# FFT convolution, one core: the inverse transform of the last two blocks with 84 stationary columns instead of 56

## The chip, the cores and the metric

One core of one Trainium2 chip. The metric is the device time of one execution in microseconds; the figures given are medians of a few executions. One further execution is recorded by the hardware profiler; its trace gives the durations and starts used below.

## The reference

A circular 7 x 7 convolution of a 224 x 224 image with 96 input and 96 output channels, written with Fourier transforms:

```
H = W = 224;  C = 96;  K = 7
x: bfloat16 (1, H, W, C);  w: bfloat16 (K, K, C, C)
wp = pad(w, to H x W)
Xf = rfft2(x, axes=(1, 2));  Wf = rfft2(wp, axes=(0, 1))      # float32
Yf = einsum('bhwi,hwio->bhwo', Xf, Wf)
y  = irfft2(Yf, s=(H, W), axes=(1, 2)).astype(bfloat16)
```

## The kernel before

The kernel does not transform the whole image. It cuts the 224 rows into NJ = 8 blocks of B = 28 rows with a halo of 6 (L = 34), and takes a short transform along the rows of each block: NS = 17 frequencies, with a real and an imaginary part, so FR = 34 numbers for each block, column and channel. Along the other axis it convolves directly. The 224 columns are done in NT = 7 tiles of 32 columns. Three kinds of work are TensorE's:

- Forward transform (`a_bank`, `f_jobs`): matmuls `pb<-Fm,xn`, 118 rows of pixels against the matrix Fm.
- The products in frequency space (`b_round`, one call for each tile and frequency): matmuls `pb<-WF,J` and `pb<-WF,xf`, 96 x 128 stationary, 96 columns of weights moving, 3,773 of them. DVE forms the operands J ahead of them (`jit`), ACT and DVE take the results out of PSUM (tiles `tt__`, `u`, `v`), POOL or DVE sum them into `yf`, and SP stores yf into a scratch tensor in DRAM (`scr`).
- Inverse transform (`c_jobs`): the scratch is read back with blocks and frequencies on the partitions (`load_t`, tiles tt), and multiplied by the inverse matrix G (named Gm in the profile). G is 102 x 84: three blocks of 34 rows by three blocks of 28 columns, zero outside the three blocks on the diagonal. ACT or DVE evict the result to a tile yo or to a part of J that is free by then, and SP writes it to the output.

The eight blocks do not divide by three. A tile has five groups (`LT`): blocks 0 to 2 and 3 to 5, each in two halves of 16 columns (gi = 0, 1), and the last two blocks, 6 and 7 (gi = 2). The last group is cut in three jobs, q = 0, 1, 2. In q = 0 and 1 the third block's place is filled with more columns of blocks 6 and 7, so these have three blocks; q = 2 has two blocks alone (`nj = 2`). Each job is a pair of matmuls (b = 0, 1), each into a PSUM bank of its own, and each followed by an eviction.

Before the change such a pair with nj = 2 loads `G[0:68, 0:56]`, 68 rows and 56 columns, and writes 56 rows of the bank. All other pairs of `c_jobs` load `G[0:102, 0:84]`. There are six pairs of the first kind, one for each of the tiles 0 to 5 (the last tile takes another way, with a matrix GY), and 60 of the second.

The order on each engine is the order in which the program issues (`_Ordered` chains the instructions of an engine). The jobs of the inverse transform are dealt out between the products of later tiles by `pace`, by the list `CQ`; most stand between a forward transform and the next products. All PSUM tiles come from eight banks in turn (`bank`). `evac` chooses ACT or DVE by a running sum of estimated costs (`load`), from the number of moving columns, not from the rows.

All instructions go through one helper line, so the profile shows line 88 for nearly all of them; the tiles' names and the shapes tell them apart.

Of the kernel before, what the change touches and what calls it, by code (L numbers as in the profile page):

```python
# [14 lines left out]
B = 28  # L15
# [40 lines left out]
def kernel(  # L56
# [7 lines left out]
    _, H, W, C = x.shape  # L64
# [6 lines left out]
    FR = 2 * NS  # L71
# [23 lines left out]
    VE, SE, GE, TE, DE = (_Ordered(e) for e in (nc.vector, nc.scalar, nc.gpsimd, nc.tensor, nc.sync))  # L95
# [9 lines left out]
    def bank():  # L105
        return pools["psb"].tile([128, 512], F32, name="pb")
# [12 lines left out]
    def evac(out_ap, in_ap, n):  # L119
        if tail[0]:  # L120
            return tail_evac(out_ap, in_ap, n)
        cv, ca = 180 + 1.0 * n, 160 + 0.85 * n
        if load["v"] + cv <= load["a"] + ca:
            load["v"] += cv
            return VE.tensor_copy(out=out_ap, in_=in_ap)
        load["a"] += ca
        return SE.copy(out=out_ap, in_=in_ap)

    def tail_evac(out_ap, in_ap, n):
        tail[0] += 1  # L130
        return VE.tensor_copy(out=out_ap, in_=in_ap) if tail[0] % 2 else SE.copy(out=out_ap, in_=in_ap)

    def dma(out_ap, in_ap):
        return DE.dma_start(out=out_ap, in_=in_ap)
# [7 lines left out]
    G = cpool.tile([3 * FR, 3 * B], BF16, name="Gm")  # L142
# [558 lines left out]
    def new_yo():  # L701
        nyo[0] += 1
        if nyo[0] % 4 > 1:
            return yo_free[nyo[0] % 4 - 2]
        return yo_pool.tile([4 * B, PXC * C], BF16, name="yo")

    def c_jobs(t):
        jobs = []
        w0 = t * 2 * TW
        for gi, h in LT:  # L710
            hold = {}
            nq = 2 if gi < 2 else 3

            def mk_(q, gi=gi, h=h, nq=nq, hold=hold):
                def put(j0, nj, px, npx, row, col):
                    dma(out[0, j0 * B:(j0 + nj) * B, w0 + px:w0 + px + npx, :].rearrange("h w c -> h (w c)"),
                        hold["yo"][row:row + nj * B, col:col + npx * C])

                def f():
                    if q % 2 == 0:  # L720
                        hold["yo"] = new_yo()
                    tt = tt_tiles[(t, gi, h)]
                    yo = hold["yo"]
                    nj = 2 if q == 2 else 3
                    for b in range(2):
                        pb = bank()[0:nj * B, 0:4 * C]
                        TE.matmul(pb, lhsT=G[0:nj * FR, 0:nj * B],
                                  rhs=tt[0:nj * FR, 4 * q + 2 * b:4 * q + 2 * b + 2, :].rearrange("p w e -> p (w e)"), start=True, stop=True)
                        k = 2 * (q % 2) + b
                        evac(yo[0:nj * B, k * 4 * C:(k + 1) * 4 * C], pb, 4 * C)  # L730
                    if q == 1 and gi < 2:
                        put(gi * 3, 3, h * PXC, PXC, 0, 0)
                    elif q == 1:
                        put(6, 2, 0, 16, 0, 0)
                        for j in range(2):
                            put(6 + j, 1, 24, 8, 2 * B, j * 8 * C)
                    elif q == 2:
                        put(6, 2, 16, 8, 0, 0)
                    if q == nq - 1:
                        held[gi == 2] -= 1  # L740
                        pump()
                return f
            for q in range(nq):
                jobs.append(mk_(q))
        return jobs
# [6 lines left out]
    def pump():  # L752
        while pend and held[pend[0][1] == 2] < (NTT, 1)[pend[0][1] == 2]:
            held[pend[0][1] == 2] += 1
            load_t(*pend.pop(0))
# [176 lines left out]
    for i, (j, h) in enumerate(order):  # L932
        if i % 4 == 0:
            yo = t_pool.tile([128, TW // 2, 2 * C], BF16, name="tt").rearrange("p w e -> p (w e)")
        second(j, h, live[(j, h)], yo)
        k = i + 8 - LF
# [38 lines left out]
```

## Time and profile before

| | |
|---|---|
| median of 3 runs | 263.42 us (263.04 to 263.55) |
| profiled execution | 263.23 us |
| its span, first to last instruction | 261.5 us |
| granted TensorE clock | 1.00 |
| matmuls `pb<-tt,Gm`, 102 rows, 84 columns | 120, 29.0 us busy |
| matmuls `pb<-tt,Gm`, 68 rows, 56 columns | 12, 3.1 us busy |
| weight loads of them | 10.4 us and 0.8 us |

In the rows of the profile "96\*128 96x96" means a stationary operand of 96 rows and 128 columns and a moving operand of 96 partitions by 96 columns. PE stands for the matmuls of TensorE, PEld for its weight loads, which can run under matmuls. The end of a matmul is modelled, so times of rows overlap; the distance from one start to the next is what a matmul takes in a stream. In the timeline the columns are start, length, engine, line, operation, operands and count, and in brackets the idle time before it with what ended it; in the list of waits they are the waiting work, what it waited for, the sum in us, how often, and the longest.

### The profile page before, as it was taken

To read this page: it belongs to the slowest core of one execution; us is meant where nothing else is said; L and a number is where in the kernel's file an instruction comes from. 1 tells how busy PE (TensorE), PEld (TensorE's weight loads), DVE (VectorE), ACT (ScalarE), POOL (GpSimd) and SP (SyncE) were. 2 spreads that over 40 slices of the span, in tenths; PEclk is the share of its full clock that TensorE was granted. 3 is DMA by queue.
4 is the path that set the end of the run, shared out by engine and by line. 5 is a ranking of instruction groups with operands and counts; after the bars stand their busy time and mean duration, and the time that the engine had idled before them with its cause. 6 is when DMAs were issued, how large, how long until landed. Compare 5 with 4: busy or idle time off the path is not lost.

```text
span 261.5 us, 12201 instructions
## 1 busy us (share of the span) xinstructions
PE 251.8 (96%) x5156; PEld 233.9 (89%) x5156; DVE 213.9 (82%) x455; ACT 198.0 (76%) x499; POOL 106.7 (41%) x172
## 2 busy tenths in 40 slices
PE   8999998999999999999999999999999999999982
PEld 3679998999999999999999989998999999999861
DVE  5659999898878889877977797777978889889982
ACT  5548997678885667997988879988798886666662
POOL 7784223435546533432243313543143222555621
PEclk9999999999999999999999999999999999999999
DMA  6848010721112399997978469797969853495145
GB/s 171 238 136 205 23 49 3 231 89 50 46 52 88 99 274 144 271 275 200 300 207 238 127 184 262 204 241 181 288 215 207 221 174 133 132 174 169 53 115 177
DMA packets 41416, 43.44 MB, mean 166 GB/s; under 512 B 30836, under 2 KB 33104, under 8 KB 41362
## 3 DMA queue, kind: packets, MB, share of 16 engines
q1 hardware_dynamic: 41044, 41.98, 58.5%
q8 instruction: 40, 0.66, 1.2%
q0 software_dynamic: 192, 0.52, 0.7%
q10 hardware_dynamic: 126, 0.17, 0.2%
q14 instruction: 14, 0.11, 0.1%
HBM read 22.09 MB, written 19.66 MB: 160 GB/s over the span
## 4 chain that ended last, share of the span: by engine, by line
PE 84%; DVE 4%; issue 4%; ACT 3%; POOL 3%; POOLq 0%; DVEq 0%; ACTq 0%
PE pb L88 84%; POOL ct L88 2%; ACT WF L88 1%; DVE xf L88 1%; DVE J L88 1%; POOL yf L88 1%; ACT xf L88 1%; DVE wq L88 1%; DVE u L88 0%; DVE v L88 0%; DVE yf L88 0%; ACT tt L88 0%; ACT J L88 0%; ACT tt__5413 L88 0%; ACT tt__1159 L88 0%
## 5 line engine op out<-in xcount | busy, mean ns | idle before, releaser
L88 PE MATMUL pb<-WF,J 96*128 96x96 bf16 x2782 | 160.4, 206 | 0.1
L88 PEld LDWEIGHTS <-J 96*128 96x128 bf16 x2782 | 136.0, 98 | 8.2 <-DVE u L88 1.5
L88 POOL TENSOR_TENSOR yf<-v,u 128x384 bf16<-128x384 f32 x70 | 69.1, 1002 | 127.2 <-issue 69.1
L88 ACT CAST xf<-pb 96x408 bf16<-96x408 f32 (+2 forms) x147 | 68.8, 486 | 9.1 <-PE pb L88 7.3
L88 PE MATMUL pb<-WF,xf 96*128 96x96 bf16 x991 | 61.4, 206 | 0.8 <-ACT xf L88 0.5
L88 DVE TENSOR_TENSOR J<-xf 96x1824 bf16<-96x1824 bf16 (+1 forms) x82 | 56.9, 732 | 0.1
L88 PEld LDWEIGHTS <-xf 96*128 96x128 bf16 x991 | 48.8, 98 | 1.4 <-ACT xf L88 0.6
L88 PE MATMUL pb<-Fm,xn 118*128 118x136 bf16 (+3 forms) x640 | 45.5, 199 | 1.4 <-DVE u L88 0.8
L88 PEld LDWEIGHTS <-xn 118*128 118x128 bf16 x640 | 30.5, 97 | 1.8 <-issue 1.8
L88 PE MATMUL pb<-tt,Gm 102*84 102x384 bf16 (+1 forms) x132 | 32.1, 326 | 0.0
L88 ACT CAST WF<-pb 96x480 bf16<-96x480 f32 (+1 forms) x57 | 28.4, 576 | 4.6 <-PE pb L88 4.5
L88 ACT CAST yo<-pb 84x384 bf16<-84x384 f32 (+1 forms) x65 | 27.8, 483 | 2.9 <-PE pb L88 2.9
L88 ACT CAST J<-pb 84x384 bf16<-84x384 f32 (+1 forms) x65 | 28.0, 484 | 2.5 <-PE pb L88 2.5
L88 DVE TENSOR_TENSOR J<-J 96x912 bf16<-96x912 bf16 (+2 forms) x41 | 22.8, 555 | 0.0
L88 PE MATMUL pb<-wq 98*128 98x120 bf16 (+1 forms) x288 | 21.4, 226 | 0.1
L88 PEld LDWEIGHTS <-wq 98*128 98x128 bf16 x288 | 19.4, 148 | 0.6 <-issue 0.6
L88 POOL TENSOR_TENSOR xn<-v,u 128x384 bf16<-128x384 f32 x12 | 10.9, 924 | 9.4 <-DVE J L88 6.4
L88 DVE CAST WF<-pb 96x480 bf16<-96x480 f32 (+1 forms) x15 | 8.8, 613 | 4.2 <-PE pb L88 4.2
L88 PE MATMUL pb<-wu 128*128 128x512 bf16 x39 | 11.0, 444 | 1.1 <-DVE ct L88 1.1
L88 PEld LDWEIGHTS <-Gm 102*84 102x84 bf16 (+1 forms) x132 | 11.1, 117 | 0.8
L88 DVE TENSOR_TENSOR yf<-v,u 128x384 bf16<-128x384 f32 x20 | 11.2, 558 | 0.7
L88 ACT COPY xf<-xf 96x816 bf16<-96x816 bf16 (+3 forms) x18 | 10.3, 630 | 0.0
(406 smaller groups left out, 252.8 us busy)
## 6 DMA issues: line engine op xcount, KB each, us to landing
scr<-yf SPq DMA_DIRECT2D x30, 288.0 KB
xn<-in_x_dram SPq DMA_DIRECT2D x12, 672.0 KB
tt<-scr SPq DMA_DIRECT2D x24, 336.0 KB
out_dram<-yo SPq DMA_DIRECT2D x12, 252.0 KB
out_dram<-J SPq DMA_DIRECT2D x12, 252.0 KB
tt<-scr SPq DMA_DIRECT2D x6, 288.0 KB
WF<-in_x_dram SPq DMA_DIRECT2D x2, 672.0 KB
scr<-yf SPq DMA_DIRECT2D x6, 192.0 KB
```

Of the source, the lines that this page charges most:

```text
L88: r = fn(*a, **k)
```

## The change

For q = 2 the matmuls load all 84 columns of the matrix, with the same 68 rows, and write 84 rows of the bank. The 28 added rows are the third block's columns against the first two blocks' rows, which are zero in G; they are not read. The evictions read the same 56 rows as before. For the other jobs nothing changes, as nj is 3 there.

```diff
                     nj = 2 if q == 2 else 3
                     for b in range(2):
-                        pb = bank()[0:nj * B, 0:4 * C]
-                        TE.matmul(pb, lhsT=G[0:nj * FR, 0:nj * B],
+                        pb = bank()[0:3 * B, 0:4 * C]
+                        TE.matmul(pb, lhsT=G[0:nj * FR],
                                   rhs=tt[0:nj * FR, 4 * q + 2 * b:4 * q + 2 * b + 2, :].rearrange("p w e -> p (w e)"), start=True, stop=True)
                         k = 2 * (q % 2) + b
-                        evac(yo[0:nj * B, k * 4 * C:(k + 1) * 4 * C], pb, 4 * C)
+                        evac(yo[0:nj * B, k * 4 * C:(k + 1) * 4 * C], pb[0:nj * B], 4 * C)
```

## The prediction

> **What bounds the kernel now.** First the page: which engine fills the span, at which clock, and who carries the chain that ended last.
>
> ```profile
> PE 251.8 (96%) x5156; PEld 233.9 (89%) x5156; DVE 213.9 (82%) x455; ACT 198.0 (76%) x499; POOL 106.7 (41%) x172
> PEclk9999999999999999999999999999999999999999
> PE 84%; DVE 4%; issue 4%; ACT 3%; POOL 3%; POOLq 0%; DVEq 0%; ACTq 0%
> ```
>
> TensorE is busy 96% of the span at the full granted clock, and it is 84% of the chain. The pairs that the change touches run from 116 us on. So second, who makes TensorE wait from 100 to 261 us:
>
> ```profile
> PE pb L88 <- ACT J L88: 0.5, 1, 0.5
> PE pb L88 <- ACT yo L88: 0.4, 1, 0.4
> PE pb L88 <- DVE xf L88: 0.3, 1, 0.3
> PE pb L88 <- DVE u L88: 0.3, 1, 0.3
> ```
>
> Four waits, 1.5 us together, none of them on a DMA. Third, the chain in order of time, where TensorE's stretches in that part are
>
> ```profile
> 104.33 52.25 PE pb L88 x1040
> ...
> 156.86 20.46 PE pb L88 x403
> ...
> 179.06 67.97 PE pb L88 x1377
> ```
>
> All six pairs (single starts: 116.58, 142.13, 168.25, 194.38, 217.93, 242.68 us) lie inside these stretches, where nothing but TensorE sets the time. The busy row cannot show what a pair costs, since the ends of matmuls are modelled, so I read starts. The timeline of TensorE around an 84-column pair (first answer) and around the last 56-column pair (second):
>
> ```profile
> 240.56 0.46 PE L88 MATMUL pb<-WF,J 96*128 96x96 bf16 x7
> 240.85 0.49 PE L88 MATMUL pb<-tt,Gm 102*84 102x384 bf16 x2
> 241.18 0.59 PE L88 MATMUL pb<-WF,J 96*128 96x96 bf16 x10
> ...
> 242.29 0.46 PE L88 MATMUL pb<-WF,J 96*128 96x96 bf16 x7
> 242.68 0.51 PE L88 MATMUL pb<-tt,Gm 68*56 68x384 bf16 x2
> 243.12 0.47 PE L88 MATMUL pb<-WF,J 96*128 96x96 bf16 x7
> ```
>
> Seven matmuls of J and a pair: from 240.56 to 241.18 it is 0.62 us, from 242.29 to 243.12 it is 0.83 us. The first column holds the whole prediction: 0.10 us are lost ahead of the pair (0.39 for seven matmuls instead of 0.29) and 0.11 behind or inside it (0.44 instead of 0.33). The weight loads say the same from the other side:
>
> ```profile
> 242.68 0.13 PEld L88 LDWEIGHTS <-Gm 68*56 68x56 bf16 x2
> 243.12 0.37 PEld L88 LDWEIGHTS <-J 96*128 96x128 bf16 x8 [0.31 <-issue]
> ```
>
> Everywhere else a load starts 1 to 2 ns after the start of the matmul ahead of it; here the first load of the pair, and the load behind the pair, come only once the matmul ahead has run out.
>
> **The gaps in ns.** From the matmul ahead of the pair, the four distances start to start are 135, 184, 258, 53 at the last pair (630 together). The 26 pairs with 84 columns between 96-column matmuls have 42, 167, 162, 45 (416, from 415 to 417). The other form: four of the six pairs stand behind a 136-column matmul of Fm; there it is 150, 183, 259, 53 (645, all four alike), and for 84 columns in that place 58, 166, 162, 45 (431 in 31 pairs, from 430 to 433). So a 56-column pair costs 214 ns more, in whichever place: about 93 on the way in, 17 between its two matmuls, 97 on the way out and 8 behind that. Both forms move 384 columns of data, and both wait on an eviction by semaphore, so neither size nor wait tells them apart. Row counts of 96, 102 and 118 follow each other all over the trace without such a gap; 84 columns beside 128 columns have none; only 56 have it, each time, going in and coming out.
>
> The Trainium skill, page "TensorEngine Tiling (Array Packing)", section "Tiling Modes" (key properties), says that a change of the tiling mode, not just of the tile, drains TensorE; up to 64 stationary columns can be run as a column tile there. By that rule the drain belongs to the 56 columns and goes with them.
>
> **The change part by part.**
> 1. The twelve matmuls take 84 columns instead of 56. If they then behave as the other 120 of that width, each pair falls to 416 or 431 ns: 4 x 214 + 2 x 214 = 1.28 us less on TensorE. Ends: nothing, if the gap belongs to the 68 rows or to this tile of data; 1.28 us if it belongs to the columns. I take the upper end, the row that has the same columns, the same data width and the same neighbours.
> 2. The weight loads grow. A load of 68x56 takes 104 ns (x12), one of 102x84 takes 118 ns (x120): 12 x 14 = 0.17 us more on PEld. It is free, because the load of an 84-column pair begins under the matmul ahead and the next matmul comes 166 ns later; if that cover were gone, 0.17 us.
> 3. Each matmul writes 28 more rows of its PSUM bank, which nobody reads. No row isolates this. The 84-row pairs, which write the same, are the nearest: 162 to 167 ns for 384 columns, and a 136-column matmul writing 128 rows takes 58 to 64. So nothing, at either end.
> 4. The evictions keep their 56 rows, order and engine; DMAs, queues and waits keep their places: in the built program DVE, ACT, POOL and SP have the same instructions in the same order, and TensorE differs only in the twelve. No wait is added.
>
> **Where the time goes then.** What is late next? The stall at 156.86 hangs on DVE, which made u after ACT had filled tt__4735; ACT waited for TensorE there:
>
> ```profile
> 154.46 0.41 ACT L88 ACTIVATE tt__4735<-pb 128x288 f32<-128x288 f32 x1 [0.99 <-PE pb L88]
> ```
>
> With TensorE 0.43 us earlier (two pairs), ACT starts that much earlier and the stall moves along whole. The stall at 179.06 hangs on ACT, which stood idle for TensorE 0.36 us at 171.35, 0.14 at 173.44 and 0.19 at 175.47 and 177.50; it moves too. At the end the last pair is followed by DVE's idle time at 243.38 (0.39, for ACT, which waited for TensorE), and the chain goes TensorE, DVE, TensorE, output. So I let all of the 1.28 us reach the end.
>
> **Sum.** The profiled execution took 263.23 us, 261.5 of it span and 1.73 around it. 263.23 - 1.28 = 261.95. The median of the runs is 263.42, 0.19 above that execution; 263.42 - 1.28 = 262.14 us is the forecast.
>
> **The rivals.**
> - Absorbed in part. A stall that runs by its own clock (a DMA, a backlog on ACT or DVE) eats what came before it: the two pairs ahead of 156.86 (0.43 us, giving 262.57), or three ahead of 179.06 (0.64, giving 262.78). For: ACT is busy 22.36 of the 26 us from 142 to 168, DVE 20.93. Against: the idle times just read, all of them waits for TensorE, and no wait of TensorE on a DMA. 6%.
> - No change: the gap belongs to the 68 rows or to the place, and stays. 263.42, or with the wider loads uncovered 263.59. For: the 56-column pairs are also the only ones with 68 rows, so this trace cannot part the two. Against: no other change of rows has a gap. 5%.
> - Slower: the gap stays, and the wider load of the second matmul is no longer taken early, so that the distance inside a pair becomes what it is on the way out, 258 instead of 184 ns. 6 x 74 = 0.44 and the 0.17 of the loads: 264.03. It decides from 88 ns more in a pair (0.53 us over six). Against: in all 57 pairs of 84 columns the second load starts under the first matmul. 4%. The Trainium skill, "TensorE: Matmul & The Clock Gate", section "LDWEIGHTS (loading the stationary operand)", speaks for this side: load time goes with the columns, at P/1.2 ns, so an estimate by it is 23 ns more for each of the twelve loads, 0.28 us; the trace has 14 ns.
>
> **How the numbers follow.** The forecast has 85%, its own range 261.85 to 262.45 (the runs of before lie from 263.04 to 263.55). To reach 8 in 10 with some room for a smaller gain, the range goes on to the worst of the absorbed cases: 261.85 to 262.8. A measurement of this kernel tells about 0.2%, 0.53 us, from no change. The forecast (1.28 us) and both absorbed cases (0.85 and 0.64) lie beyond it: 91% faster; no change 5% same; 4% slower.
>
> **What would show it.** In the profile after: twelve more matmuls pb<-tt,Gm with 84 columns and 68 rows; in the timeline the group behind each such pair 0.33 us after the pair's start; the load of J behind it starting under the second matmul; single distances of 416 or 431 ns. The span falls to about 260.2, and the chain's three stretches sum 1.28 us less, with the four waits as before. Wrong in step 1 if the group behind still comes after 0.44; wrong in the passing on if the pairs shrink and the waits at 156.9, 179 or 249 us grow by as much.

## The result, and the profile after

| | before | after | ratio of the two, with its interval |
|---|---|---|---|
| median with the first result (6 and 6 runs) | 263.26 us | 261.56 us | 0.9947 (0.9932 to 0.9961) |
| median of a later comparison (23 and 12 runs) | 262.82 us | 261.93 us | 0.9968 (0.9950 to 0.9986) |
| profiled executions | 263.23 us, span 261.5 | 261.39 us, span 259.7 | |

The kernel is faster by about 0.3 to 0.5%. The forecast ratio, 262.14 to 263.42, is 0.9951 and lies in both intervals. The two profiled executions differ by 1.84 us, more than the 1.28 us forecast; where the rest comes from is told below. The time itself, 261.56 us, lies 0.29 under the lower end of the forecast's range (261.85); by the ratio, 0.9947 x 263.42 = 262.02 us, it lies inside.

From the page of the profile after, the engines and the chain ("issue" is time in which the engine waited for nothing that the profile shows):

```profile
PE 250.1 (96%) x5156; PEld 234.3 (90%) x5156; DVE 213.8 (82%) x455; ACT 197.9 (76%) x499; POOL 107.8 (42%) x172
PE 82%; DVE 6%; issue 4%; ACT 3%; POOL 3%; DVEq 0%; POOLq 0%; ACTq 0%
```

TensorE still sets the time. Its timeline at the last of the six pairs, and the weight loads there:

```profile
240.56 0.46 PE L88 MATMUL pb<-WF,J 96*128 96x96 bf16 x7
240.86 0.49 PE L88 MATMUL pb<-tt,Gm 68*84 68x384 bf16 x2
241.19 0.59 PE L88 MATMUL pb<-WF,J 96*128 96x96 bf16 x10
```

```profile
240.82 0.16 PEld L88 LDWEIGHTS <-Gm 68*84 68x84 bf16 x2
241.03 0.64 PEld L88 LDWEIGHTS <-J 96*128 96x128 bf16 x11
```

From 240.56 to 241.19 it is 0.63 us, where it was 0.83. The first load of the pair starts 0.04 us ahead of its matmul, under the last matmul of J; the load of J behind the pair starts at 241.03, under the second matmul of the pair, 0.16 us before the matmul that uses it. Both had to wait before. In ns the four distances are 43, 166, 162 and 45 (416 together, 630 before), and 58, 166, 162 and 45 (431, from 645) at the four pairs behind a matmul of Fm.

TensorE's waits from 100 to 261 us, and its long stretches in the chain:

```profile
PE pb L88 <- ACT yo L88: 0.4, 1, 0.4
PE pb L88 <- DVE xf L88: 0.3, 1, 0.3
PE pb L88 <- DVE u L88: 0.3, 1, 0.3
```

```profile
104.38 51.81 PE pb L88 x1040
156.47 88.62 PE pb L88 x1801
...
249.33 4.68 PE pb L88 x66
```

The wait on DVE's u ends at 156.47 instead of 156.86. It moved with the two pairs ahead of it: TensorE's stretch there is 51.81 us long instead of 52.25, as forecast. The wait that was put down to "ACT J", 0.5 us before 179.06, is gone, and two stretches have become one. That was not forecast.

**Taking the noise out.** The same kernel's runs spread over more than 1 us, and the chain tells where: the stretch that begins near 104 us begins anywhere from 104.3 to 106.1 us in the profiles below, before any of the six pairs has run. The time from there to the last stretch (104.33 and 251.27 in before, 104.38 and 249.33 after) holds all six pairs and is steady. I call it the middle part.

| kernel | middle part, us | less 144.95 | six pairs, from their distances | single stops seen in it |
|---|---|---|---|---|
| after | 144.95 | 0 | 0 | none |
| after, again | 145.12 | 0.17 | 0 | 0.18 at 229.4, tt late |
| before | 146.94 | 1.99 | 6 x 0.214 = 1.28 | 0.69 at 178.3 |
| before, again | 146.24 | 1.29 | 1.28 | none |

Stops that all of them have are left out of the last column. Two profiles without a stop of their own, after and "before, again", differ by 1.29 us, and the six pairs explain 1.28.

### The profile page after: what moved, and what is told of

Its sections match the earlier page's. It is cut to its first block, busy times and chain, and to the rows that moved or that the text cites. A ratio compares the mean times of both kernels' runs of the same rounds, so it can differ in the third digit from the quotient of the medians.

```text
span 259.7 us, 12201 instructions
## 1 busy us (share of the span) xinstructions
PE 250.1 (96%) x5156; PEld 234.3 (90%) x5156; DVE 213.8 (82%) x455; ACT 197.9 (76%) x499; POOL 107.8 (42%) x172
## 4 chain that ended last, share of the span: by engine, by line
PE 82%; DVE 6%; issue 4%; ACT 3%; POOL 3%; DVEq 0%; POOLq 0%; ACTq 0%
PE pb L88 82%; POOL ct L88 2%; DVE J L88 2%; ACT WF L88 1%; DVE xf L88 1%; DVE u L88 1%; POOL yf L88 1%; DVE v L88 1%; DVE WF L88 1%; ACT xf L88 1%; DVE wq L88 1%; DVE yf L88 0%; ACT tt L88 0%; ACT tt__1860 L88 0%; ACT tt__1159 L88 0%
## 5 line engine op out<-in xcount | busy, mean ns | idle before, releaser
L88 POOL TENSOR_TENSOR yf<-v,u 128x384 bf16<-128x384 f32 x70 | 69.8, 1011 | 124.1 <-issue 67.8
```

Source lines behind the costliest of these rows:

```text
L88: r = fn(*a, **k)
```

## The experiments

The edits are shown against the kernel after. A time without a ratio is that of a single execution, so the distances and the middle parts carry the argument.

**Where the bound lies.** Two kernels differ by one stationary column in the six pairs. The first:

```diff
-                        pb = bank()[0:3 * B, 0:4 * C]
-                        TE.matmul(pb, lhsT=G[0:nj * FR],
+                        nc_ = 64 if nj == 2 else 3 * B
+                        pb = bank()[0:nc_, 0:4 * C]
+                        TE.matmul(pb, lhsT=G[0:nj * FR, 0:nc_],
```

> The six pairs load 64 of the 84 columns (68x64); evictions read 56 rows. Theory (the gap belongs to going to 64 or fewer columns and back): the gaps stay whole, 630 ns for the last two pairs and 645 for the first four, 0.33 us more on no other row; time as before, 263.3 within 0.4. Rival (the gap grows with the missing columns, 28 of 84): a third or so of it goes, 560 to 610 ns. Rival (it belongs to the 68 rows): cannot hold any more after the 84-column run, whose pairs have 68 rows and 416 and 431 ns.

The second has 65 in the place of 64.

> The six pairs load 65 columns, one more than the kernel with 64. Theory (a bound between 64 and 65 columns): 416 and 431 ns a pair, gaps gone whole, time as with 84 columns, 261.4 to 262.3. Rival (gradual): within 10 ns a pair of the kernel with 64 columns.

The timelines of TensorE at the last pair, 64 columns first:

```profile
242.11 0.46 PE L88 MATMUL pb<-WF,J 96*128 96x96 bf16 x7
242.50 0.51 PE L88 MATMUL pb<-tt,Gm 68*64 68x384 bf16 x2
242.94 0.64 PE L88 MATMUL pb<-WF,J 96*128 96x96 bf16 x11
```

```profile
241.18 0.46 PE L88 MATMUL pb<-WF,J 96*128 96x96 bf16 x7
241.48 0.49 PE L88 MATMUL pb<-tt,Gm 68*65 68x384 bf16 x2
241.81 0.76 PE L88 MATMUL pb<-WF,J 96*128 96x96 bf16 x14
```

0.83 us against 0.63. In ns: 136, 187, 258, 53 with 64 columns (634), 42, 167, 162, 45 with 65 (416). Times 263.07 and 261.93 us; middle parts 146.51 (of it 0.24 for tt that came late at 229.5) and 144.94. The bound is sharp and lies between 64 and 65 columns; the rival of a gradual price has fallen.

**Not the 68 rows.** In one kernel all 66 pairs load 56 columns; the eviction and output of the third block go with it.

```diff
-                        pb = bank()[0:3 * B, 0:4 * C]
-                        TE.matmul(pb, lhsT=G[0:nj * FR],
+                        pb = bank()[0:2 * B, 0:4 * C]
+                        TE.matmul(pb, lhsT=G[0:nj * FR, 0:2 * B],
...
-                        put(gi * 3, 3, h * PXC, PXC, 0, 0)
+                        put(gi * 3, 2, h * PXC, PXC, 0, 0)
...
```

> All 66 pairs load 56 columns; the third block of each is left out, with its 28 rows in evictions and output. Theory (214 ns for each pair, and TensorE sets the time everywhere): 60 x 0.214 = 12.8 us over before, 276 within 1. Rival (much of it hidden beside ACT and DVE, as there would be time for them): 266 to 272.

275.11 us, 12.3 over the median of before. TensorE's timeline at one pair with 102 rows:

```profile
242.34 0.51 PE L88 MATMUL pb<-tt,Gm 102*56 102x384 bf16 x2
242.79 0.34 PE L88 MATMUL pb<-WF,J 96*128 96x96 bf16 x4
```

From the pair to the group behind it are 0.45 us, where it is 0.33 with 84 columns. Pairs with 102 rows and 56 columns take 645 or 630 ns like those with 68 rows. Three pairs stand together at the end and pay for one change in and out, so 58 prices are added: 58 x 0.214 = 12.4 us. That 12.3 comes so close to 12.4 is luck, for two things cancel. Part was eaten: the stop that stands ahead of 104 us in before is 0.22 shorter, the one ahead of 156.86 0.44, and the one at 249 0.21, presumably because DVE and ACT catch up in the gaps. And this execution came late to its first pair: the matmul ahead of it starts at 103.74 us, 0.82 later than in before. From that matmul to the last stretch it takes 13.00 us more than the kernel after: the distances at the pairs grow by 13.78 (64 prices, counted against after), the stops shrink by 0.87, and 0.09 is spread over the rest. Absorption exists, then, but here it took ten times the original dose, and was 6% of it.

**Rows have a bound of their own.** With 64 instead of 68 rows and all 84 columns, so that the last four rows are left out of their sums:

```diff
-                        TE.matmul(pb, lhsT=G[0:nj * FR],
-                                  rhs=tt[0:nj * FR, 4 * q + 2 * b:4 * q + 2 * b + 2, :].rearrange("p w e -> p (w e)"), start=True, stop=True)
+                        nr_ = 64 if nj == 2 else 3 * FR
+                        TE.matmul(pb, lhsT=G[0:nr_],
+                                  rhs=tt[0:nr_, 4 * q + 2 * b:4 * q + 2 * b + 2, :].rearrange("p w e -> p (w e)"), start=True, stop=True)
```

> The six pairs load 64 rows of the matrix and 84 columns; the last 4 rows are left out of their sums. It asks whether the gap also comes with few rows. Theory (any change of the part of the array in use drains it): gaps as with 56 columns, about 630 and 645 ns a pair, time as before. Rival (the columns alone): 416 and 431, time as with 84 columns and 68 rows.

TensorE's timeline at the last pair:

```profile
243.39 0.46 PE L88 MATMUL pb<-WF,J 96*128 96x96 bf16 x7
243.78 0.52 PE L88 MATMUL pb<-tt,Gm 64*84 64x384 bf16 x2
244.23 0.94 PE L88 MATMUL pb<-WF,J 96*128 96x96 bf16 x18
```

It is 0.84 us again. The distances are 136, 195, 255 and 53 ns (639), and 150, 195, 255, 53 behind Fm. The gap is back with 84 columns. The time, 264.34 us, has 1.7 us from a late start (its stretch begins at 106.08); the middle part is 146.30, 1.35 over 144.95, and 6 x 0.223 is 1.34. So it is not the columns as such: it is a matmul of few columns (56 and 64 were run) or few rows (64) among matmuls of more. For rows the bound lies somewhere from 64 to 68. The Trainium skill, page "TensorEngine Tiling (Array Packing)", section "Tiling Modes", lists modes with 64 columns and modes with 64 rows, and says that a change of the tiling mode drains TensorE. The traces agree as far as they go: a gap at each change, about 93 ns in, and out 97 for columns, 93 for rows. No row of a trace shows the mode itself.

**One narrow matmul, or two.** The first of each pair has 56 columns, the second 84.

```diff
+                        nc_ = 2 * B if nj == 2 and b == 0 else 3 * B
+                        pb = bank()[0:nc_, 0:4 * C]
+                        TE.matmul(pb, lhsT=G[0:nj * FR, 0:nc_],
```

> In each of the six pairs the first matmul has 56 columns, the second 84. Theory (a price for each change of width, paid once going in and once coming out, however many narrow matmuls stand between): the way out moves between the two matmuls, 135 + 258 + 162 + 45 = 600 ns for the last two pairs, 615 for the first four; 0.2 us of time gained at most. Rival (a price for each narrow matmul): half of 214 goes, 523 and 538 ns, 0.64 us gained.

263.70 us; middle part 146.54, 1.59 over 144.95: the six pairs are 6 x 0.239 = 1.43, and two single stops 0.17 (0.07 at 166.2, 0.10 for a tt that came late near 230). The timeline of TensorE:

```profile
242.78 0.46 PE L88 MATMUL pb<-WF,J 96*128 96x96 bf16 x7
243.18 0.63 PE L88 MATMUL pb<-tt,Gm 68*56 68x384 bf16 x2
243.65 0.72 PE L88 MATMUL pb<-WF,J 96*128 96x96 bf16 x13
```

The distances are 135, 277, 195 and 47 ns, 655 together: half the narrow matmuls, and 25 ns more than with two. (The row shows the pair under the shape of its first matmul.) The price is one of changes, not of matmuls, so the rival has fallen; but my 600 left something out. The matmul right behind a change starts with its weight load not done ahead, and the next one is late for it: by 33 ns if an 84-column load must follow (195 instead of 162), by 8 to 11 with a load of J (53 instead of 42 to 45), by 17 inside a 56-column pair. The same 195 stands in three profiles inside the pair near 230 us, whose tt came late. So 33 ns is what a weight load of 84 columns cost here when it had lost its cover.

**Does the load's length matter while it is covered?** The matrix padded with zeros to 128 columns, loaded whole by all 132 matmuls:

```diff
-    G = cpool.tile([3 * FR, 3 * B], BF16, name="Gm")
+    Gw = cpool.tile([3 * FR, 128], BF16, name="Gm")
+    G = Gw[:, 0:3 * B]
...
+    GE.memset(Gw[:, 3 * B:], 0.0)
...
+                        pb = bank()[0:128, 0:4 * C]
+                        TE.matmul(pb, lhsT=Gw[0:nj * FR],
```

> All 132 matmuls of the inverse transform load 128 columns: the 84 of the matrix and 44 of zeros, written once by POOL at the start. Evictions read the same rows. Theory (the 8 ns that a pair of 84 columns takes over its data, 4 on the first matmul and 3 to 4 on the matmul behind the pair, are its longer weight load, 118 ns against 98 for 128 columns): they go, 66 x 8 = 0.5 us less than with 84 columns, about 261.4. Rival (the load is hidden, the 8 ns are something else): same as with 84 columns within 0.2 us.

The weight loads of the padded kernel did get shorter, 98 ns against 118 (last columns: busy us and mean ns of one, then idle time):

```profile
L88 PEld LDWEIGHTS <-Gm 102*128 102x128 bf16 x120 | 9.1, 98 | 0.3
L88 PEld LDWEIGHTS <-Gm 68*128 68x128 bf16 x12 | 0.9, 98 | 0.0
```

The pairs did not: 416 and 431 ns as with 84 columns, middle part 144.94. Median 261.73 us, ratio to before 0.9953 (0.9929 to 0.9976), no different from the 84-column kernel beside it (261.93). My theory of the 8 ns has fallen; what they are stays open.

**The stop at 178.3 us.** The kernel before, unchanged:

> The kernel before, unchanged. It asks about the stall of 0.69 us at 178.3 us that the profile of before has and that of the 84-column kernel lacks. Theory (a late fetch of TensorE's instructions, by chance of the DMA traffic): it may be absent here, the span then about 260.8, and where it is absent no fetch ends with more than 400 instructions issued since it was due; where it is present, that fetch ends beyond 400. Rival (it belongs to the kernel before, by its timing): it stands again at 178.3 with 0.69 us.

262.64 us, span 260.9, middle part 146.24. TensorE's long stretches in the chain show no stop at 178:

```profile
104.50 52.25 PE pb L88 x1040
157.03 89.48 PE pb L88 x1801
...
250.74 4.68 PE pb L88 x66
```

The kernel after, timed again:

> The kernel with 84 columns, unchanged. Theory (1.28 us from the gaps, the rest of the first difference from a stall for instructions that the profile of before had by chance): the ratio to before comes to 1.28 of 263.3, 0.9951, or 0.9949 to 0.9930 if the stall is more frequent in before; span 259.7 to 260.3 without a late fetch. Rival (the change itself removes the stall): 1.28 + 0.6, 0.9929 or less.

Ratio 0.9968, and nothing of 1.28 + 0.6. So the stop does not belong to the kernel before, and the change did not remove it. What it was, the loads of the first profile of before tell better than the waits:

```profile
177.60 0.77 PEld L88 LDWEIGHTS <-J 96*128 96x128 bf16 x14
179.04 0.17 PEld L88 LDWEIGHTS <-xn 118*128 118x128 bf16 x3 [0.67 <-issue]
```

The load waited for nothing that the trace shows; the eviction named in the list of waits had ended, by the count of ACT's increments, 2.1 us earlier. The instruction queue is the candidate:

```profile
q8 instruction: 40, 0.66, 1.2%
```

40 fetches of 16 KB, for 10,312 matmuls and weight loads, are 258 instructions a fetch. I counted how many of TensorE's instructions had begun when a fetch landed, less 256 for each fetch ahead of it (a trial value close under 258; the places of the stops, below, bear it out). In before one fetch (176.37 us, 1.33 long) landed at 422, 0.6 us ahead of the stop; the others at 374 or less. In eight profiles of the kernels above the fetch of that place landed at 244 to 322 (294 in the one after). In the one-narrow kernel a fetch landed at 401, and there TensorE stood for 75 ns at 166.2 with its semaphores long met. No fetch of the other profiles landed above 398, and from 100 us on none shows such a stop.

The place of the stops says more. When TensorE stood still, 7,361 of its instructions had begun in before and 6,849 in the one-narrow kernel. That is 512 apart, two fetches of 256, though these are different points of the kernel's work. Counted like the landings, both stops stand at 449, and TensorE went on 1.34 and 1.43 us after the landing. In the twelve profiles 468 fetches have a place 449. At two more of them TensorE stood just there, at 1,985 instructions, ahead of a matmul that waits for no semaphore: 0.28 us in the 64-column kernel and 0.05 in after, both near 52 us, and it went on 1.39 us after the landing. The weight load in the 64-column kernel:

```profile
52.70 0.39 PEld L88 LDWEIGHTS <-J 96*128 96x128 bf16 x8 [0.23 <-issue]
```

At the other 464 places TensorE went on 1.61 us or more after the landing, and no idle time is left there that the other profiles, or a change of width, do not explain. By this TensorE passes the place no sooner than about 1.4 us after the landing, and stands where it comes there earlier. To force such a stop, one more transfer was put in SP's order near 170 us, in the 84-column kernel:

```diff
             if s == 3:
                 queue_c(t - 1)
+            if t == 4 and s == 5:
+                dup = dr_pool.tile([28, W * C], BF16, name="dup")
+                dma(dup, x[0, 0:28].rearrange("h w c -> h (w c)"))
```

> The 84-column kernel with one transfer more: 28 rows of x (1.2 MB) copied from DRAM to a scratch tensor in DRAM, issued by SP near 170 us, ahead of the seventh tile's pixels. Nothing reads it. Theory (the stall of 0.69 us at 178.3 in the profile of before is a late fetch of TensorE's instructions behind DMA traffic): the fetch that starts at 172.7 with 84 columns starts later and ends after more than 400 instructions, and TensorE stands still near 178 by 0.3 us or more without a semaphore that comes late. Rival (traffic does not hold up a fetch): the fetch ends below 320 as before, and what waits there are at most the matmuls on pixels or tt that land late.

261.53 us, middle part 144.95, no stop. The fetch landed at 362, later than in those eight, but TensorE passed the place 449 only 2.19 us after that, so the fetch was 0.8 us too early for a stop. With 56 rows:

> The same with 56 rows (2.4 MB). Theory: the fetch comes later still, and the stall is longer than with 1.2 MB. Rival: no stall of this kind.

262.86 us, middle part 146.3, but by another way: the fetches landed at 326 and 352, and the traffic held up the output, so that ACT waited for a buffer and fell behind. TensorE stood five times between 191 and 195 us (1.38 us over the usual distances): four times for ACT, and the last time for DVE, which had waited 1.74 us for the store of yf. ACT's timeline:

```profile
188.77 0.85 ACT L88 CAST yo<-pb 84x384 bf16<-84x384 f32 x2 [1.83 <-DMA out_dram<-yo]
```

So the stop was not brought about, and that DMA traffic makes a fetch late is not shown. That a late fetch made the stop rests on four stops at one place, each 1.34 to 1.43 us behind a landing, against 464 fetches that came earlier and show none. It is well supported, but no edit produced it.

## Why the prediction was right, and where it was not

- **What bounds the kernel**: right. The middle part is longer or shorter by what the pairs take, within 0.02 us once single stops are counted, with 56, 64, 65, 84 and 128 columns and with 64 rows. (With 56 columns everywhere, part is eaten, as told above.)
- **Step 1, the gaps**: right in size (214 ns a pair, six pairs, 1.28 us) and in cause. The 68 rows, the open point of the no-change rival, are cleared by the 84-column kernel itself and by 102 x 56, where the gap is.
- **Step 2, the wider loads**: right that they cost nothing while covered. They take 118 ns as forecast, and the 128-column kernel moves them to 98 without any effect. The rule of the Trainium skill, page "TensorE: Matmul & The Clock Gate", section "LDWEIGHTS (loading the stationary operand)", that the time goes with the columns gave an estimate of 23 ns more a load. The trace has 14, and 98 ns for 128 columns against 118 for 84, so here the time did not go with the columns alone.
- **Step 3, rows nobody reads**: right; 128 rows instead of 84 change no distance.
- **Step 4**: right; no new wait of TensorE.
- **Where the time goes then**: right for the stall at 156.86, which moved whole. Wrong for the one at 179.06. I put it on ACT by its label and had it move along; it was a single event of that execution. The weight load beside it said "issue" with 0.67 us, and ACT's idle times just before, which I read as proof that the stall would move, were proof that ACT was not late. (The two of 0.19 us I read as waits for TensorE; the trace puts them down to ACT's own xf.) Of the 1.84 us between the two profiles, 1.28 are the pairs and 0.69 is this stop; the rest, -0.13, lies nearly all outside the middle part.
- **The sum**: right for the kernel, by the two middle parts without a stop (1.29 against 1.28) and by both ratios. The absolute forecast of 262.14 us was set against a median that may hold such stops and late starts; the later medians of before lie 0.16 and 0.60 lower. The medians alone give 1.70 us with the first result and 0.89 later, so that the 1.28 stands by the middle parts, not by them.
- **The rivals**: the slower one never came near; its condition, a second load that loses its cover, does occur in the one-narrow kernel, and costs 33 ns there, not the 74 that I had taken from the way out.

## What to carry to other kernels

When matmuls of few stationary columns or rows (56 and 64 columns and 64 rows were run here) stand alone among larger ones, read the distances from start to start on both sides: each change cost some 95 ns here, and filling up with zero columns to 65, 84 or 128 took it away at no other price. Busy times do not show it (3.1 us for the twelve narrow matmuls, 2.9 after). Before a stall is counted as moving or staying, look whether a second profile of the same kernel has it, and compare parts of the chain between two common points instead of whole spans.

## What the runs showed that I had not expected

- The price of a change does not depend on the matmul ahead: 93 ns in, behind 136 columns of data as behind 96.
- One narrow matmul beside a wide one costs more (655 ns) than two narrow ones (630).
- The first 104 us vary from one execution to the next by up to 1.7 us, more than the whole effect; the part after that repeats to some hundredths once single stops are taken off.
- A stop that the list of waits puts down to ACT can be none of ACT's: in four profiles TensorE stood at the same place of a fetch of its instructions, for 0.05 to 0.69 us, with no semaphore that came late.
